# A linear-attention and MLP kernel: the MLP's weights read with strides of 1 to 5 elements

## The chip, the cores and the metric

The kernel runs on one core of one Trainium2 chip. The metric is the device time of one execution in microseconds; smaller is better. Before the change two runs gave 878.12 and 878.20 us, median 878.16.

## The reference

Two layers, each linear attention followed by an MLP, both behind a layer norm and added to the residual; both layers use the same weights. 2048 tokens, D = 448, 16 heads of 28, F = 1792.

```python
def attn(x, wqkv, wo):
    q, k, v = split_heads(x @ wqkv)
    phi = lambda t: where(t > 0, t + 1, exp(t)) + 1e-6
    kv = einsum("bhsd,bhse->bhde", phi(k), v)
    z = phi(k).sum(tokens)
    o = (phi(q) @ kv) / (phi(q) . z + 1e-6)
    return merge_heads(o) @ wo

def mlp(x, w1, b1, w2, b2):
    return gelu_tanh(x @ w1 + b1) @ w2 + b2

x = A_x
for _ in range(2):
    x = x + attn(layernorm(x), wqkv, wo)
    x = x + mlp(layernorm(x), w1, b1, w2, b2)
```

## The kernel before

Everything is float32 outside; matmuls run in a rounded float32 type, and to keep the precision each operand is split in a high and a low part, so that a product takes three matmuls (high x high, high x low, low x high). The last 64 rows of D = 448 have both parts stacked on 128 partitions, so their product takes two matmuls. The 2048 tokens are 16 tiles of 128, and 4 tiles make a block.

A layer has two phases. Phase 1 goes over the 16 tiles: layer norm, transposes, K and Q projections, and the sum of phi(k) times the normalised rows. A short transition makes the attention's per-head matrices from it. Phase 2 is the loop `for b in range(NB)` over the 4 blocks, inside it `for i in range(NF)` over 14 chunks of 128 of the 1792 MLP features. All orders are written out by hand; nothing is scheduled by a tool. In the loop TensorE does in turn `mlp1(l, b, i + 1)`, the pieces of the next block's attention that the lists `PLAN_0`, `PLAN_1` and `PLAN` name, and `mlp2(l, b, i, acc)`.

`mlp1` (L796) multiplies one chunk of w1, the stationary operand (the weights that are loaded into the array), by the block's 512 normalised tokens, the moving operand: three rows of three matmuls at L802 to L804 and two at L805 and L806, 128 x 512 each. ScalarE (ACT) then applies gelu with the bias column from `b1s` (L808) into `g`, casts it to the high part `gh` (L811), and VectorE (DVE) subtracts to get the low part `gl` (L812). In `g`, `gh` and `gl` a partition is a feature and the 512 elements along it are the block's tokens in order, tile after tile.

`mlp2` (L815) turns it round: a 128 x 128 piece of `gh` or `gl`, the features by the tokens of tile j, is the stationary operand, and the moving one is the chunk's 128 rows of w2, 448 wide (L820 to L822). It adds up over the 14 chunks in four banks `acc`, one for each tile.

So in both halves each matmul is preceded by its own weight load, which the profile lists as engine PEld beside PE. In `mlp1` a load reads 128 neighbouring elements of a row of `w1h`, `w1l` or `w1x` in each partition; in `mlp2` 128 neighbouring elements of `gh` or `gl`.

In layer 0 the weights of the MLP are fetched in the background: `bg_pieces` (L325) loads w1 in 16 pieces and w2 in 14 of 128 rows (L350), through SyncE's (SP's) queue; ACT rounds them to the high part, GpSimd (POOL) subtracts to get the low part. `biases` (L928) loads b1 by one DMA into `b1s`, a partition for each feature of a chunk and a column for each chunk, and b2 into `b2b`. SP issues all DMAs in the order of the program.

Of the kernel before, what the change touches and what calls it, by code (L numbers as in the profile page):

```python
# [11 lines left out]
AF = mybir.ActivationFunctionType  # L12
# [10 lines left out]
def linear_attn_mlp_kernel(  # L23
# [12 lines left out]
    pe, act, dve, pool, sp = nc.tensor, nc.scalar, nc.vector, nc.gpsimd, nc.sync  # L36
# [25 lines left out]
    def bank(tag, bufs, name):  # L62
        return psum.tile([128, 512], F32, name=name, tag=tag, bufs=bufs)
# [3 lines left out]
    def t448(tag, bufs, name, dt=F32):  # L67
        bufs = NH if tag == "H" else bufs
        return work.tile([128, D], dt, name=name, tag=tag, bufs=bufs)

    def t512(tag, bufs, name, dt=F32):
        return work.tile([128, 512], dt, name=name, tag=tag, bufs=bufs)

    def f(ap):
        return ap.bitcast(F32)
# [12 lines left out]
    def stage_piece(src, c, eng, s):  # L88

        if c < 3:  # L90
            eng.dma_start(s, src[c * 128:(c + 1) * 128, :])
        else:
            eng.dma_start(s[0:64], src[TL:D, :])
            eng.dma_start(s[64:128], src[TL:D, :])
        return s
# [79 lines left out]
    b1s = consts.tile([128, NF], F32, name="b1s")  # L175
# [6 lines left out]
    w2h = wts.tile([128, NF, D], F32R, name="w2h")  # L182
    w2l = wts.tile([128, NF, D], F32R, name="w2l")
# [3 lines left out]
    def table(func):  # L187

        act.activation(none, tiny, func)
# [132 lines left out]
        return into  # L322


    def bg_pieces():  # L325
        n = 0

        def stage():
            nonlocal n
            n += 1  # L330
            if n <= LATE:
                return t512("xn", 2, "stg")[:, :D]
            return t448(f"W{5 + n % 2}", 1, "stg")

        for fc in range(4):
            sl = slice(fc * D, (fc + 1) * D)
            for c in range(4):
                s = stage_piece(w1[:, sl], c, sp, stage())

                def go(c=c, s=s, sl=sl):  # L340
                    if c < 3:
                        act.copy(w1h[:, c, sl], s)
                        pool.tensor_tensor(w1l[:, c, sl], s, f(w1h[:, c, sl]), op=OP.subtract)
                    else:
                        act.copy(w1x[:, sl], s)
                        pool.tensor_tensor(w1x[64:128, sl], s[64:128], f(w1x[64:128, sl]), op=OP.subtract)
                yield go
        for i in range(NF):
            s = stage()
            sp.dma_start(s, w2[i * 128:(i + 1) * 128, :])  # L350

            def go(i=i, s=s):
                act.copy(w2h[:, i], s)
                pool.tensor_tensor(w2l[:, i], s, f(w2h[:, i]), op=OP.subtract)
            yield go
# [4 lines left out]
    def background(n, m=NF):  # L360

        for g in bg_wait[:m]:
            bg_wait.pop(0)()
        for _ in range(n):
            g = next(bg, None)
            if g is not None:
                bg_wait.append(g)
# [425 lines left out]

    gs = {}

    def mlp1(l, b, i):  # L796
        hp = bank("h", 2, "hp")
        s = slice(i * 128, (i + 1) * 128)
        x = blocks["m", l, b]
        o = hp.rearrange("p (t n) -> p t n", t=4)  # L800
        for c in range(3):
            pe.matmul(o, w1h[:, c, s], x.moving(x.hi, c), start=(c == 0), stop=False)  # L802
            pe.matmul(o, w1l[:, c, s], x.moving(x.hi, c), start=False, stop=False)  # L803
            pe.matmul(o, w1h[:, c, s], x.moving(x.lo, c), start=False, stop=False)  # L804
        pe.matmul(o, w1x[:, s], x.moving(x.hi, 3), start=False, stop=False)  # L805
        pe.matmul(o, w1x[:, s], x.moving(x.lo, 3), start=False, stop=True)  # L806
        g = t512("e", 3, "g")
        act.activation(g, hp, AF.Gelu_apprx_tanh, bias=b1s[:, i:i + 1])  # L808
        gh = t512("A", 2, "gh", F32R)
        gl = t512("B", 2, "gl", F32R)  # L810
        act.copy(gh, g)  # L811
        dve.tensor_sub(gl, g, f(gh))  # L812
        gs[i] = (gh, gl)

    def mlp2(l, b, i, acc):  # L815
        gh, gl = gs.pop(i)
        first, last = i == 0, i == NF - 1
        for j in range(4):
            s = slice(j * 128, (j + 1) * 128)
            pe.matmul(acc[j], gh[:, s], w2h[:, i], start=first, stop=False)  # L820
            pe.matmul(acc[j], gh[:, s], w2l[:, i], start=False, stop=False)  # L821
            pe.matmul(acc[j], gl[:, s], w2h[:, i], start=False, stop=last)  # L822
            if last:
                t = b * 4 + j
                xs = xt.pop((l, t))
                dve.tensor_tensor(xs, acc[j], xs, op=OP.add)
                sp.dma_start(x_d[l + 1][t * 128:(t + 1) * 128, :], xs)
# [93 lines left out]
    for l in range(LAYERS):  # L921
        tr = SimpleNamespace(mp={})
        za, acc = phase1(l, tr)
        if l == 0:
            background(0)
        fill = list(range(DEFER, NT))

        def biases(j):  # L928
            if l == 0:
                sp.dma_start(b1s, b1.rearrange("(c p) -> p c", p=128))  # L930
                sp.dma_start(b2b, b2[None, :].to_broadcast([128, D]))

        def pre(j):
            for k in range(4):
                load_pq(l, 1, k)
            if l == 0:
                background(2)

        tok_ = SimpleNamespace(
            Q=lambda j: stage_q(l, fill.pop(0)), Qp=lambda j: fill_qphi(), Qv=lambda j: stage_qphi(j or 9),  # L940
            Qa=lambda j: stage_q(l, fill.pop(0), tag="acc"), G=lambda j: stage_g(l, NT - 1, acc),
            ld=lambda j: (load_pq(l, 0, j), load_x(l, j)), z=lambda j: trans_z(tr, za), gt=lambda j: trans_gt(tr, acc),
            kv=lambda j: trans_kv(tr), mask=lambda j: trans_mask(tr), m=lambda j: trans_m(tr, j),
            ms=lambda j: trans_ms(tr, j), qz=lambda j: q_z(l, 0, j, tr), qs=lambda j: q_scale(l, 0, j, tr),
            tq=lambda j: q_transpose(l, 0, j), qq=lambda j: q_split(l, 0, j), o=lambda j: o_mm(l, 0, j, tr),
            la=lambda j: o_ln(l, 0, j), lb=lambda j: o_n(l, 0, j), T=lambda j: m_transpose(l, 0, j),
            x=lambda j: m_split(l, 0, j), tu=lambda j: turn(xns.pop(("m", l, j)), ("m", l, 0), j),
            st=lambda j: store_sq(("m", l, 0), 0), sp=lambda j: spread(("m", l, 0), 0), pre=pre, b=biases)
        for tok in ORDER.split():
            name, j = tok.rstrip("0123456789"), int("0" + tok.lstrip("abcdefghijklmnopqrstuvwxyzQTG"))  # L950
            getattr(tok_, name)(j)
        assert not fill and not qo
        table(AF.Gelu_apprx_tanh)
        q_z(l, 1, 0, tr)
        mlp1(l, 0, 0)
        trans_chunks(tr)
        for b in range(NB):
            acc = [bank("acc", 4, f"y{j}")[:, :D] for j in range(4)]
            nxt = b + 1 < NB
            if not nxt and l + 1 < LAYERS:  # L960
                st_k = stage_square(wqkv[:, D:2 * D])
                st_q = stage_square(wqkv[:, :D])
                load_to(l + 1, PRE - 1)
            for i in range(NF):
                if i + 1 < NF:
                    mlp1(l, b, i + 1)
                elif nxt:
                    mlp1(l, b + 1, 0)
                if l == 0 and b == 0 and i:
                    background(1, 1)  # L970
                if i == NF - 2 and not nxt and l + 1 < LAYERS:
                    table(AF.Exp)
                if 9 <= i < 13:
                    add_bias(l, b, i - 9)
                if nxt:
                    behind(l, b, i, tr)
                elif l + 1 < LAYERS:
                    if i == 2:
                        split_kq("k", st_k)
                    if i == 5:  # L980
                        split_kq("q", st_q)
                    if i in (3, 4, 6, 7, 8):
                        t = (3, 4, 6, 7, 8).index(i)
                        stage_a(l + 1, t)
                        stage_n(l + 1, t)
                        stage_t(l + 1, t)
                        if t % 2:
                            stage_sp(l + 1, t)
                    if 9 <= i < 13:
                        stage_x(l + 1, i - 9)  # L990
                mlp2(l, b, i, acc)
# [28 lines left out]
```

## Time and profile before

| | us |
|---|---|
| median of two runs | 878.16 |
| the profiled execution | 878.62 |
| its span, first to last instruction | 876.9 |

The profile is of one execution. Each row of its groups has the line, the engine, the operation, the tiles (written <- read), the shapes and the count; behind the bar the busy time in us and the mean of one in ns, then the engine's idle time just ahead of these instructions and what ended it. A timeline row has the start and the duration in us ahead of the engine. The matmuls' ends are modelled and overlap the next start, so that the pace of TensorE is the distance of two starts, not the duration.

The loop over blocks and chunks lies between about 140 and 442 us in layer 0 and between about 570 and 875 us in layer 1. The mean granted clock of TensorE is 1.000. Share of busy time in some stretches of that loop:

| stretch, us | PE | PEld | DVE | ACT | POOL | DMA |
|---|---|---|---|---|---|---|
| 197 to 295 | 100% | 88% | 61% | 32% | 25% | 32% |
| 295 to 393 | 100% | 88% | 35% | 30% | 10% | 26% |
| 642 to 740 | 100% | 88% | 52% | 29% | 14% | 32% |

The 14 loads of w2 at L350 take 0.35 us each to issue and 3.0 us to land; the one of b1 takes 0.43 us to issue, at 112.8 us, and 3.8 us to land.

### The profile page before, as it was taken

What the parts mean: (1) busy time and instruction counts of PE and PEld (TensorE: products, weight loads), DVE (VectorE), ACT (ScalarE), POOL (GpSimd) and SP (SyncE); (2) the same over time, 40 slices, a digit from 0 to 9 for tenths busy, and PEclk for the clock granted to TensorE, in tenths of its full rate; (3) what the DMA queues carried; (4) which work ended last, traced back from release to release, by engine and by line L of the source; (5) the groups of instructions that cost most, each with busy time, mean ns of one, the idle gap of its engine ahead of it and who ended that gap; (6) DMA issues with size and microseconds to landing.
All of it is one profiled execution on the core that took longest, in us unless ns stands there. A gap on an engine that the chain in (4) does not pass through costs nothing.

```text
span 876.9 us, 11676 instructions
## 1 busy us (share of the span) xinstructions
PE 870.9 (99%) x4182; PEld 771.9 (88%) x4182; DVE 489.9 (56%) x953; ACT 343.5 (39%) x603; POOL 220.9 (25%) x250
## 2 busy tenths in 40 slices
PE   9999999999999999999999999999999999999998
PEld 8989888888888888888899998888888888888887
DVE  6878585658455443226467875864674473433112
ACT  5677635324223322333355665332233133223221
POOL 5566532335012102011222344120220140140000
PEclk9999999999999999999999999999999999999999
DMA  5475636623313402051145443262332413111001
GB/s 158 133 227 166 208 88 203 191 87 131 132 59 104 156 0 97 1 179 49 48 136 186 168 131 106 98 186 81 106 112 91 132 69 118 49 49 41 2 1 43
DMA packets 63482, 94.76 MB, mean 108 GB/s; under 512 B 8896, under 2 KB 58560, under 8 KB 63424
## 3 DMA queue, kind: packets, MB, share of 16 engines
q1 hardware_dynamic: 63424, 94.01, 33.5%
q8 instruction: 33, 0.54, 0.3%
q14 instruction: 25, 0.20, 0.1%
HBM read 56.17 MB, written 34.60 MB: 104 GB/s over the span
## 4 chain that ended last, share of the span: by engine, by line
PE 97%; DMA 1%; DVE 0%; POOL 0%; SPq 0%; issue 0%; ACT 0%; POOLq 0%; DVEq 0%
PE y L822 10%; PE y L820 10%; PE y L821 10%; PE hp L803 9%; PE hp L804 9%; PE hp L802 9%; PE hp L806 3%; PE hp L805 3%; PE psq L307 2%; PE psk L308 2%; PE psq L309 2%; PE psq L308 2%; PE psk L309 2%; PE G L483 2%; PE psk L307 2%; PE G L482 2%
## 5 line engine op out<-in xcount | busy, mean ns | idle before, releaser
L812 DVE TENSOR_TENSOR gl<-g,gh 128x512 fp32r<-128x512 f32 x112 | 83.1, 742 | 300.7 <-ACT gh L811 300.7
L808 ACT ACTIVATE g<-hp,b1s 128x512 f32<-128x512 f32 x112 | 77.2, 689 | 406.2 <-PE hp L806 402.7
L822 PE MATMUL y<-w2h,gl 128*128 128x448 f32 x448 | 163.7, 365 | 0.0
L821 PE MATMUL y<-w2l,gh 128*128 128x448 f32 x448 | 163.6, 365 | 0.0
L820 PE MATMUL y<-w2h,gh 128*128 128x448 f32 x448 | 163.6, 365 | 0.0
L803 PE MATMUL hp<-XH,w1l 128*128 128x512 f32 x336 | 131.5, 392 | 0.0
L802 PE MATMUL hp<-XH,w1h 128*128 128x512 f32 x336 | 131.2, 391 | 0.0
L804 PE MATMUL hp<-XL,w1h 128*128 128x512 f32 x336 | 131.2, 391 | 0.0
L204 POOL TENSOR_TENSOR brs<-bve,mhalf 128x1 f32<-128x1 f32 x64 | 39.5, 618 | 283.8 <-DVE bve L202 280.7
L820 PEld LDWEIGHTS y<-w2h,gh 128*128 128x128 f32 x448 | 84.1, 188 | 9.0
L821 PEld LDWEIGHTS y<-w2l,gh 128*128 128x128 f32 x448 | 84.1, 188 | 8.4
L822 PEld LDWEIGHTS y<-w2h,gl 128*128 128x128 f32 x448 | 84.2, 188 | 6.6
L804 PEld LDWEIGHTS hp<-XL,w1h 128*128 128x128 f32 x336 | 63.1, 188 | 14.1 <-issue 0.6
L803 PEld LDWEIGHTS hp<-XH,w1l 128*128 128x128 f32 x336 | 63.1, 188 | 11.3
L802 PEld LDWEIGHTS hp<-XH,w1h 128*128 128x128 f32 x336 | 63.1, 188 | 10.9
L811 ACT CAST gh<-g 128x512 fp32r<-128x512 f32 x112 | 69.6, 622 | 3.6
L695 POOL TENSOR_TENSOR pz<-pq,zb 128x448 f32<-128x448 f32 x32 | 36.7, 1150 | 86.4 <-DVE dn L701 75.5
L417 POOL TENSOR_TENSOR xnl<-x,xnh 128x384 fp32r<-128x384 f32 x32 | 35.1, 1097 | 70.8 <-ACT xnh L416 38.8
L297 DVE TENSOR_TENSOR XL<-sp,XH 128x512 fp32r<-128x512 f32 x50 | 44.4, 894 | 3.8 <-ACT XH L296 3.8
L806 PE MATMUL hp<-XL,w1x 128*128 128x512 f32 x112 | 43.6, 389 | 0.0
L805 PE MATMUL hp<-XH,w1x 128*128 128x512 f32 x112 | 43.6, 389 | 0.0
L764 POOL TENSOR_TENSOR x<-x,b2b 128x448 f32<-128x448 f32 x32 | 41.9, 1332 | 0.0
(146 smaller groups left out, 1563.9 us busy)
## 6 DMA issues: line engine op xcount, KB each, us to landing
x<-in_A_x_dram SPq DMA_DIRECT2D x32, 224.0 KB, 3.6
pq_d<-eq SPq DMA_DIRECT2D x32, 224.0 KB, 2.9
pq<-pq_d SPq DMA_DIRECT2D x32, 224.0 KB, 3.2
sq_m<-sq SPq DMA_DIRECT2D x14, 512.0 KB, 2.8
sp<-sq_m SPq DMA_DIRECT2D x56, 128.0 KB, 2.8
x<-x_d SPq DMA_DIRECT2D x32, 224.0 KB, 3.3
sq_a<-sq SPq DMA_DIRECT2D x12, 512.0 KB, 2.9
sp<-sq_a SPq DMA_DIRECT2D x48, 128.0 KB, 3.1
```

Source lines behind the costliest of these rows:

```text
L297: eng.tensor_tensor(lo.rearrange("p (c i n) -> p c i n", c=4, n=32), x, f(h), op=OP.subtract)
L802: pe.matmul(o, w1h[:, c, s], x.moving(x.hi, c), start=(c == 0), stop=False)
L803: pe.matmul(o, w1l[:, c, s], x.moving(x.hi, c), start=False, stop=False)
L804: pe.matmul(o, w1h[:, c, s], x.moving(x.lo, c), start=False, stop=False)
L805: pe.matmul(o, w1x[:, s], x.moving(x.hi, 3), start=False, stop=False)
L806: pe.matmul(o, w1x[:, s], x.moving(x.lo, 3), start=False, stop=True)
L808: act.activation(g, hp, AF.Gelu_apprx_tanh, bias=b1s[:, i:i + 1])
L811: act.copy(gh, g)
L812: dve.tensor_sub(gl, g, f(gh))
L820: pe.matmul(acc[j], gh[:, s], w2h[:, i], start=first, stop=False)
L821: pe.matmul(acc[j], gh[:, s], w2l[:, i], start=False, stop=False)
L822: pe.matmul(acc[j], gl[:, s], w2h[:, i], start=False, stop=last)
```

## The change

Three things are dealt out differently; what is computed and the order of all instructions stay.

*Features.* A chunk of 128 features is no longer 128 neighbours. The 1792 features are cut in four ranges, and in a range of s chunks chunk r takes the features first + r, first + r + s, first + r + 2s and so on: s = 4 for chunks 0 to 3, 3 for chunks 4 to 6, 2 for chunks 7 and 8, 5 for chunks 9 to 13. The weight loads of `mlp1` read `w1h`, `w1l` and `w1x` with that stride; w1 itself lies in SBUF as before. The rows of w2 that are loaded for a chunk are those of the same features, so that `w2h` and `w2l` are again contiguous in SBUF. `b1s` is filled by four DMAs, one for each range, of s neighbouring values for each partition, where it was one of single values.

*Tokens.* Gelu writes its 512 results in another order, which depends on the block (`tokens`): in block 0 as before; in block 1 in pairs of tiles, the tokens of the two tiles alternating; in blocks 2 and 3 the tokens of all four tiles alternating. `gh` and `gl` keep that order, and the weight loads of `mlp2` pick the tokens of one tile out of it with a stride of 1, 2, 4 and 4 elements in blocks 0 to 3.

```diff
+    SPAN = [(first, r, s) for first, s in ((0, 4), (512, 3), (896, 2), (1152, 5)) for r in range(s)]
+
+    def dealt(i):
+        first, r, s = SPAN[i]
+        return slice(first + r, first + r + 127 * s + 1, s)
+
     def bg_pieces():
...
         for i in range(NF):
             s = stage()
-            sp.dma_start(s, w2[i * 128:(i + 1) * 128, :])
+            sp.dma_start(s, w2[dealt(i), :])
...
+    def tokens(g, b):
+
+        s = (1, 2, 4, 4)[b]
+        if s == 1:
+            return g.rearrange("p (t n) -> p t n", t=4)
+        if s == 4:
+            return g.rearrange("p (n t) -> p t n", t=4)
+        return g.rearrange("p (u n t) -> p u t n", u=2, t=2)
+
     def mlp1(l, b, i):
         hp = bank("h", 2, "hp")
-        s = slice(i * 128, (i + 1) * 128)
+        s = dealt(i)
...
-        act.activation(g, hp, AF.Gelu_apprx_tanh, bias=b1s[:, i:i + 1])
+        act.activation(tokens(g, b), hp.rearrange("p (u t n) -> p u t n", u=2, t=2) if b == 1 else hp.rearrange("p (t n) -> p t n", t=4), AF.Gelu_apprx_tanh, bias=b1s[:, i:i + 1])
...
         for j in range(4):
-            s = slice(j * 128, (j + 1) * 128)
-            pe.matmul(acc[j], gh[:, s], w2h[:, i], start=first, stop=False)
-            pe.matmul(acc[j], gh[:, s], w2l[:, i], start=False, stop=False)
-            pe.matmul(acc[j], gl[:, s], w2h[:, i], start=False, stop=last)
+            h, lo = (tokens(x, b)[:, j] if b != 1 else tokens(x, b)[:, j // 2, j % 2] for x in (gh, gl))
+            pe.matmul(acc[j], h, w2h[:, i], start=first, stop=False)
+            pe.matmul(acc[j], h, w2l[:, i], start=False, stop=False)
+            pe.matmul(acc[j], lo, w2h[:, i], start=False, stop=last)
...
         def biases(j):
             if l == 0:
-                sp.dma_start(b1s, b1.rearrange("(c p) -> p c", p=128))
+                for i, (first, r, s) in enumerate(SPAN):
+                    if r == 0:
+                        sp.dma_start(b1s[:, i:i + s], b1[first:first + 128 * s].rearrange("(p c) -> p c", c=s))
                 sp.dma_start(b2b, b2[None, :].to_broadcast([128, D]))
```

## The prediction

> **What bounds the kernel now.** I read the page from the top: busy shares, then the chain of waits, the costliest groups, and the timeline of TensorE inside the MLP and at the start of the run.
>
> ```profile
> PE 870.9 (99%) x4182; PEld 771.9 (88%) x4182; DVE 489.9 (56%) x953; ACT 343.5 (39%) x603; POOL 220.9 (25%) x250
> ...
> PE 97%; DMA 1%; DVE 0%; POOL 0%; SPq 0%; issue 0%; ACT 0%; POOLq 0%; DVEq 0%
> ...
> L808 ACT ACTIVATE g<-hp,b1s 128x512 f32<-128x512 f32 x112 | 77.2, 689 | 406.2 <-PE hp L806 402.7
> L822 PE MATMUL y<-w2h,gl 128*128 128x448 f32 x448 | 163.7, 365 | 0.0
> ...
> L803 PE MATMUL hp<-XH,w1l 128*128 128x512 f32 x336 | 131.5, 392 | 0.0
> ...
> L820 PEld LDWEIGHTS y<-w2h,gh 128*128 128x128 f32 x448 | 84.1, 188 | 9.0
> ```
>
> TensorE is the whole chain. Each matmul has its own weight load (4182 of both), and the loads' rows sit almost end to end as well. The durations overlap (365 ns for a matmul that is followed sooner than that), so the pace has to be taken from starts. In block 3 of layer 0, one place where `mlp1` ends and `mlp2` begins:
>
> ```profile
> 417.58 0.39 PE L804 MATMUL hp<-XL,w1h 128*128 128x512 f32 x1
> 417.81 0.39 PE L805 MATMUL hp<-XH,w1x 128*128 128x512 f32 x1
> 418.03 0.39 PE L806 MATMUL hp<-XL,w1x 128*128 128x512 f32 x1
> 418.26 0.36 PE L820 MATMUL y<-w2h,gh 128*128 128x448 f32 x1
> 418.46 0.37 PE L821 MATMUL y<-w2l,gh 128*128 128x448 f32 x1
> 418.67 0.36 PE L822 MATMUL y<-w2h,gl 128*128 128x448 f32 x1
> ```
>
> `mlp1` goes at 228 ns a matmul (0.22 to 0.23 here), `mlp2` at 203 ns (0.20 to 0.21): over all starts of L802 to L806 and of L820 to L822 the means are 228 and 203. The load of the next weights starts as each matmul starts:
>
> ```profile
> 418.26 0.19 PEld L821 LDWEIGHTS y<-w2l,gh 128*128 128x128 f32 x1
> 418.46 0.19 PEld L822 LDWEIGHTS y<-w2h,gl 128*128 128x128 f32 x1
> ```
>
> Its row of 188 ns looks as if it almost fills the 203, but two other places show that the array is held for less. In the timeline of the start a load that has no matmul to hide behind stretches its matmul from 0.365 to 0.47 us:
>
> ```profile
> 3.20 2.79 PE L157 MATMUL warm<-ones 128*128 128x128 f32 x13
> ...
> 7.33 0.47 PE L307 MATMUL psk<-wk,XH 128*128 128x448 f32 x1 [0.45 <-ACT XH L260]
> ```
>
> And in the chain of waits, in order of time, four transposes, each with a load of 128 columns, pass in 0.44 us:
>
> ```profile
> 115.90 3.01 PE mp L652 x8
> ...
> 134.00 0.44 PE tp L247 x4
> ```
>
> So a load costs about 0.47 - 0.365 = 105 ns, and load after load goes at 0.44 / 4 = 109 ns or so with its hand-over. Hidden behind 203 ns it has 94 ns to spare, behind 228 ns 119.
>
> **The change part by part.** Counts first: 112 chunks (14 x 4 blocks x 2 layers) of 11 matmuls in `mlp1` and 12 in `mlp2`, 1232 and 1344. By weights: of `mlp1`, 4 + 5 of 14 chunks are read with a stride of 4 or 5 elements, 792 matmuls; 3 chunks with 3, 264; 2 chunks with 2, 176. Of `mlp2`, block 0 stays contiguous, block 1 reads every second element (336 matmuls), blocks 2 and 3 every fourth (672). No matmul is added, dropped or reordered; the built PE list has as many rows as before.
>
> *A strided weight load.* No row of this trace reads weights with a stride, so I bound it. Below: 109 ns, as now; a stride cannot make the load shorter than the contiguous row, so there is no gain. Above: the dearest pace of any PE row, `mp` at L652, 3.01 / 8 = 376 ns, 3.45 times 109. In the middle lies what this same load did in the first microseconds, where 13 of the warm-up's L157 took 2.79 us, 215 ns each, twice the usual time, for whatever reason. A load k times as dear costs nothing until 109 k passes the matmul's pace: k = 1.86 in `mlp2`, k = 2.09 in `mlp1`. I take k = 2 for steps of 4 and 5 elements (16 and 20 bytes) and 1 to 1.5 for 2 and 3, and choose it by the warm-up row, a load at half its rate. Then a pair takes 109 x 2 = 218 ns: `mlp1` still hides it (228), `mlp2` of blocks 2 and 3 does not: 672 x (218 - 203) ns = 10.1 us. What is late next is nothing but TensorE itself: every matmul behind moves by the same amount.
>
> [...]
>
> *Gelu's output dealt (L808).* The write to `g` gets steps of 2 or 4 elements. Bounds: nothing to a doubling, 0 to +689 ns; I take 300 (no row of ACT writes with a stride). ACT is idle 3.6 us ahead of each gelu, and from the end of `gl` to its first matmul the trace has 3.0 us in most chunks, so even +689 is hidden. The cover is thin at the last chunk of block 3 in each layer, where no next `mlp1` stands between: 0.57 us. There a doubling would show 0.12 us, twice in the run: 0 to 0.24 us, taken as 0. The cast L811 and the subtraction L812 stay contiguous.
>
> *b1 by four DMAs in place of one.* SP issued the one in 0.43 us at 112.8. Three more at 0.43 make 1.3 us; they also land in fewer, longer pieces. Behind them on SP are `b2b`, issued over by 115.0, and then the store of `pq_d` at 116.43, which waits for its data until then: the 1.4 us of gap take it. If that cover is gone, the store and what SP issues behind it move by up to 1.3 us. First use of `b1s` is 142.1. Cost 0, bound 1.3 us.
>
> *w2's rows dealt (14 DMAs).* Still 128 rows of 1792 bytes, each from another place. They land in 3.0 us now and the `w2l` made of them is ready 11.7 us or more before L821 reads it. Bounds 0 and, if a landing were doubled, 3 us in those 11.7: 0.
>
> Sum: profiled execution 878.6 us (span 876.9 and 1.7 around it) + 10.1 = 888.7; the median of the runs is 0.5 lower, 878.2, which gives 888 us, 1.1% more.
>
> **The rivals.**
>
> *No price at all (k under 1.86).* A load that takes 109 ns of a 203 ns slot has room, and TensorE reads moving data at 25 ns per 64 columns (228 - 203 ns for 512 against 448), 2.5 elements a ns, against 128 / 109 = 1.2 of a load: the port may well have that second half in hand. Time 878.2. Against it: nothing in the trace reads with a step. Chance 0.25.
>
> *The dear load binds `mlp1` too (k over 2.1).* This is the one on the other side. The point where it decides is sharp: at a pair of 229 ns `mlp2`'s strided half costs 672 x 26 = 17.5 us, just 2% of 878, and from there on the 792 matmuls of `mlp1` join, so that each further 10 ns cost 14.6 us. At k = 2.5 (272 ns): 672 x 69 + 792 x 44 = 46 + 35 = 81 us, 960 us. At the L652 pace (376 ns): 116 + 117 = 233 us, 1111 us. [...] Against it: the only load of this form that the trace shows slower than 109 ns stands at 2. Chance 0.45, of which 0.24 up to k = 2.5 and 0.21 above.
>
> *Steps of 2 and 3 pay the same as 4.* At k = 2 block 1's 336 matmuls add 336 x 15 ns = 5.0 us, 893 us; `mlp1` hides them. It lies with the forecast in its class, and its chance is in the forecast's.
>
> *ACT becomes late.* It would need a gelu 3.0 us longer than 0.69, over five times; only the two last chunks could show it. Chance negligible. That the strides vanish in building is excluded by the list of instructions only as far as counts go; if they did, the time is 878.
>
> **How the numbers follow.** Forecast (k from 1.86 to 2.1, 878 to 896 us) 0.28, no price 0.25, dear load 0.45; 0.02 for something shorter that I don't see. 2% of 878.2 is 17.6 us, about what a measurement of this kernel can tell from no change: within it (861 to 896) lie the first two, 0.53; slower 0.45; faster 0.02. The forecast is the likeliest single case, narrow as it is: 888. For 8 in 10 the range goes from just under the time of now, 877, to k = 2.5, 960: left out are 0.21 above that. The cases within 2% alone span 877 to 896.
>
> **What would show it.** Starts of L802 and of L820 (their new lines), by block and by chunk. Right: `mlp1` at 228 ns in all chunks, `mlp2` at 203 in blocks 0 and 1 and near 218 in blocks 2 and 3; block time of 2 and 3 longer by 168 x 15 ns = 2.5 us each. No price: 203 everywhere. The dear load: chunks 0 to 3 and 9 to 13 of every block slower than chunks 4 to 8, and blocks 2 and 3 far above 218. Gelu's row in blocks 1 to 3 against block 0 shows the price of its strided write, and any idle time of PE with ACT or DVE as releaser would make the argument on slack wrong. A weight-load row that stays at 188 ns while the pace changes would show that the row's length is no measure of the load.

## The result, and the profile after

The changed kernel takes 912.08 us (two runs, 911.80 and 912.36) against 878.16: a ratio of 1.0386 with a 95% interval of 1.0342 to 1.0431. The profiled execution has a span of 910.1 us against 876.9, 33.2 us more.

The page of the changed kernel has the same engine at the end of everything; the rows that moved are the weight loads and, off the path, gelu. Columns as before: busy us and mean ns behind the bar.

```profile
PE 904.6 (99%) x4182; PEld 857.2 (94%) x4182; DVE 487.4 (54%) x953; ACT 371.8 (41%) x603; POOL 221.1 (24%) x250
...
PE 96%; DMA 1%; DVE 1%; ACT 1%; issue 0%; SPq 0%; POOL 0%; DVEq 0%; ACTq 0%; POOLq 0%
...
L824 ACT ACTIVATE g<-hp,b1s 128x512 f32<-128x512 f32 x112 | 105.6, 943 | 411.7 <-PE hp L822 408.7
...
L838 PE MATMUL y<-w2h,gl 128*128 128x448 f32 x448 | 171.1, 382 | 0.0
...
L838 PEld LDWEIGHTS y<-w2h,gl 128*128 128x128 f32 x448 | 117.0, 261 | 2.7
...
L819 PEld LDWEIGHTS hp<-XH,w1l 128*128 128x128 f32 x336 | 95.3, 284 | 1.4
```

Counts and order are those of before; loads that took 188 ns now average 261 and 284. The timeline of TensorE in block 3 of layer 0, where chunk and tokens both have a step of 4 or 5, shows what follows from it (start and duration in us):

```profile
441.63 0.40 PE L821 MATMUL hp<-XH,w1x 128*128 128x512 f32 x1
441.87 0.40 PE L822 MATMUL hp<-XL,w1x 128*128 128x512 f32 x1
442.11 0.36 PE L836 MATMUL y<-w2h,gh 128*128 128x448 f32 x1
442.31 0.40 PE L837 MATMUL y<-w2l,gh 128*128 128x448 f32 x1
442.54 0.40 PE L838 MATMUL y<-w2h,gl 128*128 128x448 f32 x1
442.78 0.40 PE L836 MATMUL y<-w2h,gh 128*128 128x448 f32 x1
```

and the weight loads of the same stretch:

```profile
442.11 0.31 PEld L837 LDWEIGHTS y<-w2l,gh 128*128 128x128 f32 x1
442.32 0.33 PEld L838 LDWEIGHTS y<-w2h,gl 128*128 128x128 f32 x1
442.56 0.33 PEld L836 LDWEIGHTS y<-w2h,gh 128*128 128x128 f32 x1
442.79 0.33 PEld L837 LDWEIGHTS y<-w2l,gh 128*128 128x128 f32 x1
```

`mlp2` now starts a matmul every 0.23 us, not 0.20; a load starts 0.01 us behind the matmul ahead and the next matmul 0.22 us behind the load. It is the load that sets the pace. (The load's row of 0.33 us is longer than that distance, so its length is no measure of the time that a load takes; the pace is read from starts.) `mlp1` stands at 0.24. Summed over the distances of all starts in the two traces:

| matmuls | step | count | before, ns | after, ns | us more |
|---|---|---|---|---|---|
| `mlp2`, block 0 | 1 | 336 | 202.8 | 203.1 | 0.1 |
| `mlp2`, block 1 | 2 | 336 | 202.7 | 203.6 | 0.3 |
| `mlp2`, blocks 2 and 3 | 4 | 671 | 202.7 | 232.9 | 20.2 |
| `mlp1`, chunks 7, 8 | 2 | 176 | 228.5 | 233.0 | 0.8 |
| `mlp1`, chunks 4 to 6 | 3 | 264 | 228.5 | 235.0 | 1.7 |
| `mlp1`, chunks 0 to 3 | 4 | 352 | 228.9 | 238.7 | 3.4 |
| `mlp1`, chunks 9 to 13 | 5 | 440 | 228.1 | 239.9 | 5.2 |
| all other | 1 | 1606 | 197.9 | 198.9 | 1.6 |

In the rows of `mlp1` these are means over a chunk's 11 matmuls. The 1.6 us of the last row are 1.8 more in phase 1 of layer 1, 0.4 less in phase 1 of layer 0 and 0.2 more in the loops.

### The profile page after: what moved, and what is told of

It is laid out like the page before. It is cut to its first block, busy times and chain, and to the rows that moved or that the text cites. A ratio compares the mean times of both kernels' runs of the same rounds, so it can differ in the third digit from the quotient of the medians.

```text
span 910.1 us, 11679 instructions
## 1 busy us (share of the span) xinstructions
PE 904.6 (99%) x4182; PEld 857.2 (94%) x4182; DVE 487.4 (54%) x953; ACT 371.8 (41%) x603; POOL 221.1 (24%) x250
## 4 chain that ended last, share of the span: by engine, by line
PE 96%; DMA 1%; DVE 1%; ACT 1%; issue 0%; SPq 0%; POOL 0%; DVEq 0%; ACTq 0%; POOLq 0%
PE y L838 11%; PE y L837 11%; PE y L836 11%; PE hp L818 9%; PE hp L820 9%; PE hp L819 9%; PE hp L821 3%; PE hp L822 3%; PE psq L307 2%; PE psq L309 2%; PE psq L308 2%; PE psk L308 2%; PE G L490 2%; PE G L491 2%; PE psk L309 2%; PE G L489 2%
## 5 line engine op out<-in xcount | busy, mean ns | idle before, releaser
L824 ACT ACTIVATE g<-hp,b1s 128x512 f32<-128x512 f32 x112 | 105.6, 943 | 411.7 <-PE hp L822 408.7
L838 PE MATMUL y<-w2h,gl 128*128 128x448 f32 x448 | 171.1, 382 | 0.0
L837 PE MATMUL y<-w2l,gh 128*128 128x448 f32 x448 | 170.9, 381 | 0.0
L836 PE MATMUL y<-w2h,gh 128*128 128x448 f32 x448 | 169.3, 378 | 0.0
L837 PEld LDWEIGHTS y<-w2l,gh 128*128 128x128 f32 x448 | 116.0, 259 | 3.9
L838 PEld LDWEIGHTS y<-w2h,gl 128*128 128x128 f32 x448 | 117.0, 261 | 2.7
L836 PEld LDWEIGHTS y<-w2h,gh 128*128 128x128 f32 x448 | 115.7, 258 | 2.8
L818 PEld LDWEIGHTS hp<-XH,w1h 128*128 128x128 f32 x336 | 94.9, 282 | 2.0
L819 PEld LDWEIGHTS hp<-XH,w1l 128*128 128x128 f32 x336 | 95.3, 284 | 1.4
L820 PEld LDWEIGHTS hp<-XL,w1h 128*128 128x128 f32 x336 | 93.7, 279 | 2.2 <-issue 0.3
```

What stands on the lines that cost most here:

```text
L824: act.activation(tokens(g, b), hp.rearrange("p (u t n) -> p u t n", u=2, t=2) if b == 1 else hp.rearrange("p (t n) -> p t n", t=4), AF.Gel ...
L836: pe.matmul(acc[j], h, w2h[:, i], start=first, stop=False)
L837: pe.matmul(acc[j], h, w2l[:, i], start=False, stop=False)
L838: pe.matmul(acc[j], lo, w2h[:, i], start=False, stop=last)
```

## The experiments

The theory after this reading: a strided weight load takes longer by itself, some 233 ns at a step of 4, and the matmul waits for it wherever it is the shorter of the two. The rivals: the two halves disturb each other; transfers or gelu are behind it; or a strided read takes a fixed time from the stream of the moving operand.

**Tokens alone.** The features, the rows of w2 and b1 as before the change.

```diff
...
-        s = dealt(i)
+        s = slice(i * 128, (i + 1) * 128)
...
```

> Gelu's tokens dealt by 1, 2, 4, 4 and read as strided weights in mlp2; the features of w1, the rows of w2 and b1 as before the change. Load-bound theory (a weight load with a step of 4 elements takes some 233 ns start to start, and a matmul of 448 columns, 203 ns, waits for it): mlp2 at 233 ns in blocks 2 and 3, 205 or less in block 1, 203 in block 0, mlp1 back at 228 ns everywhere; 878.2 + 672 x 30 ns + 336 x 1 ns = 899 us. Rival (the two halves slow each other down, so one half alone costs far less than its share of the 34 us): under 890 us.

903.44 us, ratio 1.0286 (1.0269 to 1.0303). `mlp2` at 234 and 235 ns in blocks 2 and 3, 203.7 in block 1. `mlp1` was back at 229 ns in blocks 0 and 1 but at 231 in blocks 2 and 3, which I had not expected (231 is one of the paces of the last section). 21.4 us lie in blocks 2 and 3 of `mlp2`, so this half has its price by itself; the 4 us above my figure are its 234 to 235 ns in place of 233 (1.2 us), `mlp1` (2.1 us) and what lies outside the MLP (1.3 us).

**Features alone.** Gelu and `mlp2` contiguous.

```diff
...
-            h, lo = (tokens(x, b)[:, j] if b != 1 else tokens(x, b)[:, j // 2, j % 2] for x in (gh, gl))
+            h, lo = (tokens(x, 0)[:, j] for x in (gh, gl))
```

> The features dealt with strides of 4, 3, 2 and 5, with the rows of w2 and the four DMAs of b1; gelu and mlp2 contiguous as before the change. If mlp1's extra 5 to 12 ns a matmul come from its own strided loads: mlp1 at 233 (step 2), 235 (3), 238 (4), 240 ns (5), mlp2 203 everywhere, 878.2 + 1232 x 10 ns = 891 us. Rival (mlp1's extra is a knock-on of mlp2's late loads or of the dealt order of gelu): mlp1 at 228, 879 us.

889.85 us, ratio 1.0129 (1.0114 to 1.0144); `mlp1` at 233, 235, 238 and 240 ns by step as in the whole change, `mlp2` at 203. After the first matmul of a chunk with step 4 or 5 the next one starts 261 ns later on average. That first matmul's load started with the last matmul of `mlp2` and had only its 203 ns to hide behind, which is 30 short of 233. The two halves, 25.2 and 11.6 us, make 36.8; together they cost 33.9. They add up, but for 3 us.

**Transfers alone.** All weights contiguous, gelu in order; rows of w2 and b1 as in the change.

> Only the transfers of the change: rows of w2 dealt and b1 by four DMAs, all weights read contiguously and gelu in order (w1's chunk and w2's rows are then not the same features, so the MLP's product is another one). If the transfers cost nothing: 878 us. Rival: they delay a stage, 880 us or more.

878.26 us in a single run, beside 878.25 before; every mean of the table above is back at its value of before to 0.1 ns. No cost is seen.

**Gelu's write alone.**

> Gelu writes with steps of 2 and 4 in blocks 1 to 3, the transfers are those of the change, and all weights are read contiguously (so the tokens come out in another order). If the gelu of 1182 ns in place of 689 is hidden: 878 us, mlp1 228 and mlp2 203 everywhere. Rival (ACT's slower write delays mlp2 or slows TensorE's reads): mlp1 or mlp2 slower in blocks 2 and 3, 881 us or more.

880.93 us in a single run, beside 878.65: almost the 881 of the rival. But `mlp1` and `mlp2` hold 228 and 203 ns in all blocks, so the slower write takes nothing from TensorE's reads. The last chunk of block 3 shows the thin cover that the prediction named:

```profile
440.67 0.69 DVE L828 TENSOR_TENSOR gl<-g,gh 128x512 fp32r<-128x512 f32 x1 [3.65 <-ACT gh L827]
...
441.42 0.19 PEld L838 LDWEIGHTS y<-w2h,gl 128*128 128x128 f32 x1 [0.17 <-DVE gl L828]
```

The load waits for `gl`, and one matmul starts 69 ns late (62 in layer 1). That is not 2 us. Most of the rest, 1.8 us, is in phase 1 of layer 1, whose lines nobody changed: there the kernel before goes at 202.7 ns a matmul, this one at 206.7, for some 440 matmuls from the late one on. Another 0.6 us is in phase 1 of layer 0, ahead of any gelu.

**A grid of widths.** The sharpest one: shorten the moving operand until only the load is left.

```diff
...
+            n = 4 - b
+            m = 4 if c == 0 else n
+            pe.matmul(o[:, :m], w1h[:, c, s], x.moving(x.hi, c)[:, :m], start=(c == 0), stop=False)
...
+            w = D - 64 * (i // 2)
+            pe.matmul(acc[j][:, :w], h, w2h[:, i, :w], start=first, stop=False)
...
```

> Parts of the product are left out so that the pace of a load shows by itself: mlp1's matmuls take 512, 384, 256 and 128 moving columns in blocks 0 to 3 (the first row of three of each chunk's first matmul stays at 512), mlp2's 448 down to 64 in steps of 64 over pairs of chunks; the features are dealt with steps 1, 2, 3, 4, 4. To be read from the starts, not from the total. Load-bound theory: with a step of 4 the period stays at about 233 ns at every width up to 448; with a step of 1 it falls by 0.417 ns a column to a floor of 109; step 2 has a floor near 115 and step 3 one near 174 (from the longer rows of their loads, 194 and 253 against 188). Rival (a strided load takes a fixed time away from the moving stream): the period is that of step 1 plus a fixed 31 ns (mlp2, step 4) or 6 to 10 ns (mlp1) at every width, so 140 ns at most at 128 columns.

Medians of the distance between starts in `mlp2`, by the step of block 0, 1 and 3:

| moving columns | step 1 | step 2 | step 4 |
|---|---|---|---|
| 384 | 174 | 173 | 233 |
| 320 | 147 | 147 | 233 |
| 256 | 120 | 120 | 234 |
| 192 | 112 | 119 | 235 |
| 128 | 112 | 119 | 233 |
| 64 | 112 | 118 | 233 |

Step 3, in `mlp1` of the same run: 178 at 384 columns, 174 at 256, 175 at 128. The load-bound theory holds within 4 ns of its floors (109, 115, 174 and 233), step 1 falls by 27 ns for 64 columns from 384 to 256, 0.42 a column, and the rival, 140 ns at most at 128 columns, is out: with step 4 a matmul of 64 columns takes as long as one of 384. At 448 columns step 4 stood at 238 ns, and at 373 where the granted clock was 0.50; matmuls of 448 columns with contiguous loads stand at 373 there too, so there the load is the shorter of the two. The timeline of step 1 at 192 columns:

```profile
193.78 0.27 PE L840 MATMUL y<-w2l,gh 128*128 128x192 f32 x1
193.89 0.27 PE L841 MATMUL y<-w2h,gl 128*128 128x192 f32 x1
194.00 0.28 PE L839 MATMUL y<-w2h,gh 128*128 128x192 f32 x1
```

and of step 4 at 128 columns:

```profile
417.58 0.43 PE L841 MATMUL y<-w2h,gl 128*128 128x128 f32 x1
417.81 0.43 PE L839 MATMUL y<-w2h,gh 128*128 128x128 f32 x1
418.04 0.43 PE L840 MATMUL y<-w2l,gh 128*128 128x128 f32 x1
418.28 0.43 PE L841 MATMUL y<-w2h,gl 128*128 128x128 f32 x1
```

The floors 119, 175 and 233 are close to 2, 3 and 4 times 58 ns: from step 2 to step 4 each step adds 56 to 58 ns. The 112 ns of step 1 do not fit this (58). What the price comes from is not shown.

**Steps of 8 and 5.** The same grid with other steps.

> The same grid of widths, the features now dealt with steps of 8 (chunks 0 to 7), 5 (8 to 12) and 1 (13); parts of the product are left out as in the grid before. [...] At 128 columns, where the granted clock drops, step 1 should be far below 233 unless the clock doubles its load.

At 512, 384, 256 and 128 columns (medians from a chunk's fifth matmul on): step 5 gives 236, 231, 227 and 226 ns, step 8 gives 243, 240, 240 and 240. The price does not go on growing with the distance: another 57 ns a step, an estimate from the grid's 119 and 233, would make 290 at step 5 and 461 at step 8. Steps 4, 5 and 8 lie at 233, 226 and 240; what makes these three differ stays open. Step 1 at 128 columns stood at 213, in stretches where the granted clock was 0.50.

**Steps of 2 everywhere.** All 14 chunks are dealt in pairs, and the tokens with steps of 1, 2, 2 and 2.

```diff
-    SPAN = [(first, r, s) for first, s in ((0, 4), (512, 3), (896, 2), (1152, 5)) for r in range(s)]
+    SPAN = [(first, r, s) for first, s in ((0, 2), (256, 2), (512, 2), (768, 2), (1024, 2), (1280, 2), (1536, 2)) for r in range(s)]
...
-        s = (1, 2, 4, 4)[b]
+        s = (1, 2, 2, 2)[b]
...
```

> [...] Rival (any step but 1 slows the matmul by some fixed time, and 4 and 5 merely by more): mlp2 above 208 in blocks 2 and 3, over 890 us.

887.28 us, ratio 1.0101 (1.0084 to 1.0118): `mlp2` 203.5 ns, `mlp1` 233. The load of 119 ns at step 2 is hidden in both halves, as the load-bound theory has it. By the table of the changed kernel, with 0.9 ns more in `mlp2` and 4.5 in `mlp1` at step 2, the sum is 878.65 + 1008 x 0.9 + 1232 x 4.5 ns = 885.1 us; phase 1 of layer 1, at 206.7 ns again, gives 1.8 us that it does not have. The rival (over 890, `mlp2` over 208) is out.

**Tokens by three.** Three tiles' tokens alternate in blocks 2 and 3, the fourth stays together; the features are those before the change. The diff is against the changed kernel.

```diff
...
-            h, lo = (tokens(x, b)[:, j] if b != 1 else tokens(x, b)[:, j // 2, j % 2] for x in (gh, gl))
+            h, lo = (x[:, 384:] if j == 3 else x[:, :384].rearrange("p (n t) -> p t n", t=3)[:, j] for x in (gh, gl)) if b > 1 else (tokens(x, b)[:, j] if b != 1 else tokens(x, b)[:, j // 2, j % 2] for x in (gh, gl))
...
```

> As the run with the tokens alone, but in blocks 2 and 3 the tokens of three tiles alternate (step 3) and those of the fourth tile stay together; gelu is two instructions there, and all output is computed. [...] Rival (the price grows evenly with the step and falls on the matmul, two thirds of step 4's 30 ns at step 3): mlp2 near 223, 672 x 3/4 x 20 ns = 10 us, 889 us.

883.84 us, ratio 1.0063 (1.0046 to 1.0080), 19.6 us less than with step 4. Of the 6.3 us that the profiled span is longer than before (883.2 against 876.9), 2.5 lie outside the MLP and 2.2 in `mlp1`, at 231 ns in blocks 2 and 3 as with step 4. `mlp2` in block 3 is at 0.20 to 0.21 us, 205 ns on average:

```profile
420.57 0.36 PE L841 MATMUL y<-w2h,gh 128*128 128x448 f32 x1
420.77 0.36 PE L842 MATMUL y<-w2l,gh 128*128 128x448 f32 x1
420.97 0.37 PE L843 MATMUL y<-w2h,gl 128*128 128x448 f32 x1
421.18 0.37 PE L841 MATMUL y<-w2h,gh 128*128 128x448 f32 x1
```

The edge lies between 3 and 4, where the load's 175 and 233 ns stand on either side of the matmul's 203. A price that grows evenly with the step and falls on the matmul would have given 223.

**The moving operand in one run.** Why do steps 2 and 3, whose loads are hidden, cost `mlp1` 5 and 7 ns?

```diff
-            return x.rearrange("p (t c n) -> p t c n", t=4, c=4)[:, :, c]
+            return x[:, c * 512:(c + 1) * 512].rearrange("p (t n) -> p t n", t=4)
```

> As the changed kernel, but mlp1's moving operand is one run of 512 neighbouring elements in place of four runs of 128 (it then multiplies other tokens and rows than it should). It asks where mlp1's 5 to 7 ns come from at steps of 2 and 3, whose loads of 119 and 175 ns are hidden. If the moving stream and the strided load get in each other's way at the jumps between runs: mlp1 back at 228 with steps 2 and 3, 233 with 4 and 5; about 904 us. Rival (the jumps have nothing to do with it): 233 and 235 as before, 912 us.

911.55 us in a single run, `mlp1` at 233 and 235 as before: the jumps between the runs of 128 have nothing to do with it.

**Widths near 512.**

> Parts of the product are left out: mlp1's moving operand is one run of 512, 480, 448 and 416 columns in blocks 0 to 3, the features are dealt with steps 1, 1, 2, 3, 4, 3, and gelu and mlp2 are contiguous. It asks whether the 5 to 8 ns that steps 2 and 3 cost at 512 columns are a cost of the load or a matter of how load and matmul fall into step. A cost of the load: the same 5 ns (step 2) and 8 ns (step 3) above step 1 at every width. A matter of step: the differences change from width to width, with 0 or less at some and up to 8 at others, while step 4 stays at 233 at all four.

Medians at 512, 480, 448 and 416 columns: step 1 227, 217, 206, 189; step 2 233, 215, 202, 187; step 3 235, 220, 203, 195; step 4 237, 235, 238, 233. Step 2 is 6 ns dearer than step 1 at 512 and 2 to 4 cheaper at the other three; step 3 is 8 and 3 above, then 3 below, then 6 above. Step 4 is up to 5 ns over the 233 expected. So it is no fixed cost of the load. My reading, which no run isolates, is that the matmuls fall into one of several paces a few ns apart, and a changed load shifts which. The kernel before has such paces too: of the 1232 distances of its `mlp1`, 836 are 226 or 227 ns and 243 are 231 or 233. What picks the pace stays open.

## Why the prediction was wrong

*What bounds the kernel, and the counts:* right. TensorE is still the chain, and the table above goes by the same numbers of matmuls.

*The strided load:* the step that failed is "I take k = 2 [...] Then a pair takes 109 x 2 = 218 ns: `mlp1` still hides it (228)". The mechanism was the right one, a load that `mlp2` cannot hide; the size was not. The load takes 233 ns from start to start, k = 2.14, just past the point of 229 ns that the prediction gives for the other case. So `mlp2`'s term was 20.2 us for the 10.1 forecast, and `mlp1`, put at nothing, gave 11.1. The second rival, the dear load that binds `mlp1` too, is what happened, at its lower end. Its own formula at 233 ns makes 672 x 30 + 792 x 5 ns = 24.1 us, 902 us. The missing 10 us are the first load of each dear chunk, hidden behind 203 ns only (72 x 30 ns = 2.2 us), another 3 to 5 ns in the rest of those chunks (3.0 us), 2.5 us in steps 2 and 3, 1.6 us outside the MLP and 0.4 in `mlp2` of blocks 0 and 1.

The choice of k had no row behind it of a strided read. The warm-up row that I leaned on was a contiguous load at 215 ns. The grid has contiguous loads at 213 ns where the granted clock is 0.50, a clock that the strided load does not follow (below); at the warm-up the profile before shows no such clock (1.00 from 3.20 to 6.00 us), so why that row was slow is not shown. With the outcome decided by 11 ns, between 218 and 229, the 888 us were a guess at one side of an edge, and by the prediction's own chances the less likely side: 0.28 against 0.45 for the dear load. The range, 877 to 960, did hold the time.

*Steps of 2 and 3:* right for `mlp2` (203.6 at step 2, and 202 to 205 in the tiles with step 3 in the run by three). For `mlp1` the prediction had 228 ns; 233 and 235 came, by paces that nothing in it foresaw.

*Gelu:* its write went from 689 to about 719 ns at step 2 and 1182 at step 4, inside the bounds of 0 to +689: the +493 at step 4 lies midway between the 300 taken and the upper bound. In the changed kernel it was hidden, at the last chunk too, where `mlp2` itself goes at 233 ns. With gelu's write alone it showed at the thin place, by 69 and 62 ns where the bound was 120. By the cover of 0.57 us that the prediction gave, +493 would have shown nothing: that cover runs to the start of the matmul, and in the profile before the load that reads `gl` starts 0.20 us ahead of it.

*b1 and the rows of w2:* right, nothing.

*No price at all:* out. *ACT becomes late:* only with gelu's write alone, at the last chunk of each layer.

## What to carry to other kernels

A weight load that hides behind its matmul has a reserve; work it out from starts, and set against it what a strided load takes here: 119, 175 and 233 ns for 128 float32 elements at steps of 2, 3 and 4, and 226 to 240 at 5 and 8. A layout that leaves the stationary operand with a step of 2 or 3 cost about 1% or less in this kernel; one with a step of 4 cost 3% for half of one product. Where a forecast hangs on which side of an edge an unmeasured price falls, a row of another kind does not settle it: say the edge, give each side its sum, and forecast by the side that your own chances favour.

## What the runs had that I had not expected

The load with a step of 4 does not follow TensorE's granted clock. In the grid the granted clock drops in some stretches of short matmuls; the stretch that holds the 128-column rows shown above (columns: busy us and counts by engine, then the clock, DMA share and GB/s):

```profile
410.00:425.00 15.00, 15.00 (x64) 14.85 (x64) 6.30 (x9) 7.00 (x9) 4.69 (x4) 0.50 0.11 35
```

At a clock of 0.50 step 4 stays at 233 ns, as it does at 1.00 (block 2 of the grid from 300 to 338 us, 384 to 192 columns; 232.9 in the changed kernel), while contiguous loads go from 112 to 213. So the granted clock does not set the limit of the strided load at step 4. What sets it is not shown.

The stream of matmuls has more than one steady pace for the same work. Phase 1 of layer 1, kernel before:

```profile
479.77 0.37 PE L307 MATMUL psq<-wq,XH 128*128 128x448 f32 x1
479.97 0.36 PE L308 MATMUL psq<-wq,XH 128*128 128x448 f32 x1
480.18 0.36 PE L309 MATMUL psq<-wq,XL 128*128 128x448 f32 x1
480.38 0.36 PE L311 MATMUL psq<-wq,XH 128*128 128x448 f32 x1
```

and with gelu's write alone:

```profile
481.20 0.37 PE L307 MATMUL psq<-wq,XH 128*128 128x448 f32 x1
481.41 0.37 PE L308 MATMUL psq<-wq,XH 128*128 128x448 f32 x1
481.61 0.37 PE L309 MATMUL psq<-wq,XL 128*128 128x448 f32 x1
481.82 0.37 PE L311 MATMUL psq<-wq,XH 128*128 128x448 f32 x1
```

In nanoseconds the distances repeat as 199, 207, 202, 203, 202 in the first, mean 202.7, and as 207, 207, 206 in the second, mean 206.7, for some 440 matmuls on end. The changed kernel and all seven runs in which gelu is dealt (tokens alone, tokens by three, steps of two, gelu's write alone, the moving operand in one run, and the two grids of widths with steps up to 4 and 8) went through this phase at 206.7; the kernel before and the three with gelu in order (the features alone, the transfers alone, the widths near 512) at 202.7.

That looks like an effect of gelu, but the same two paces stand in phase 1 of layer 0, between about 53 and 92 us, ahead of every instruction of TensorE and ACT that was changed. There the tokens alone, the features alone, the tokens by three, the moving operand in one run and the widths near 512 went at 206.7, and the others, the kernel before and the changed one among them, at 202.7. Being late is no sure way in either: with gelu's write alone the slower pace began at the late matmul in layer 0, but the eight matmuls that follow the late one in layer 1 go at the faster pace. So no cause of the pace is shown, and up to 2 us of difference between these kernels can come from it.
